# Block attention and soft mixture of experts: scores from four 64x64 parts of the array, in a PSUM layout of fixed bank pairs

## The chip, the cores and the metric

The kernel runs on one core of a Trainium2 chip. The metric is the device time of one execution in microseconds (us). Before the change it is 252.64 us, the median of 3 runs (252.4 to 253.21). The engines have the names of the profile: PE is TensorE's matmul and PEld its weight load, DVE is VectorE, ACT is ScalarE, POOL is GpSimd, SP is SyncE, which issues the transfers (SPq is its queue).

## The reference

Everything is float32. Stage one is attention within chunks of 64 tokens, for 8 batches of 8 heads with 576 tokens and head size 64. Stage two is a soft mixture of 8 experts with 4 slots each on the 4608 token rows of 512.

```python
# attention, per batch, head and chunk of 64 tokens
scores = scale * (q_c @ k_c.T);  scores -= scores.max(-1)
attn = exp(scores) / (sum(exp(scores)) + 1e-9)
x = (attn @ v_c)                      # as rows: (4608, 512)
# soft mixture: 32 slots
logits = x @ phi                      # (4608, 32)
d = softmax of logits over all rows;  slot_input = d.T @ x
slot_out[e] = relu(slot_input[e] @ w1[e]) @ w2[e]
c = softmax of logits over the slots; return c @ slot_out
```

## The kernel before

The order of the work is written out by hand, and every engine takes its instructions in the order of the code. The program puts in the waits: an instruction waits where it touches a tile that another engine still writes or reads, and for a PSUM tile that holds between two readers too.

Stage one goes through 36 steps `t` (9 batches of four pairs of heads; the ninth "batch" is the last 64 tokens of all eight). A step covers 512 tokens of two heads, that is 16 blocks of 64 tokens. Its work is cut into parts that a loop (from `for t in range(NT - 2)` on) runs staggered, so that one pass holds parts of five steps:

- `s1(t)`, scores: 8 matmuls into the PSUM tile `psc` (L193). Keys lie in `qkT` twice, each time with the other head's 64 partitions zeroed (memsets L404 and L405), so one matmul contracts over all 128 partitions and gives both heads' scores of one block. Then DVE: maximum `mx` (L201), subtraction into `sc` (L203).
- every fourth pass, `logits`, `weights`, `sums`: the token logits `pl` of a finished batch (L271), their running maximum `nm_run` (L285, L286), exponentials `eT` (L289), a copy `lT` (L299) and a factor `al` (L294) on ACT.
- `transposes(t + 2)`: 8 transposes of queries and keys into the pair of banks `pqk` (L166), then four copies out into `qkT`: three on ACT (L181), the fourth on DVE (L179).
- every fourth pass, one pass after the logits, `partial`: `pp`, the slots' partial sums (L351), and their addition into `p_run` on DVE (L364).
- `s3(t - 3)`: 4 transposes of the results `x` into `px` (L254), and a copy into `xT`, on DVE (L259) in even steps up to `t` = 28, on ACT (L261) in the others.
- `s2a(t - 1)`: 4 transposes of the exponentials into `pt` (L216), a copy into `at` on ACT (L218).
- in the passes with logits, `natural`: two transposes `pe` (L313, L315), a copy `eN` on ACT (L317), then `cm` and `c_all` on DVE (L328, L329).
- `s1b(t)`: the exponential of the scores on ACT (L208).
- `s2b(t - 2)`: 16 matmuls of 64x64 with the values into the pair of banks `pav` (L234); on DVE the reciprocals `rc` (L241, L242) and the product `x` (L243).

After the loop (34 passes) the last parts follow in an order of their own; then the slots' inputs, the experts' two products (`ph` L571, `po` L603) and the combination (`pf` L638) make the second half. It opens PSUM and most of SBUF anew, and its weights `w` are loaded into buffers that stage one's tiles free.

PSUM has eight banks of 512 floats per partition. Stage one spends them in two pools: four single banks that go round over `psc`, `px`, `pt`, `pl`, `pe` and `pp`, and two pairs that go round over `pqk` and `pav`. Since these two take turns, each of them has in effect one pair.

Of the kernel before, what the change touches and what calls it, by code (L numbers as in the profile page):

```python
# [16 lines left out]
def kernel(  # L17
# [81 lines left out]
    with ExitStack() as actx:  # L99
        ap_ = actx.enter_context(tc.tile_pool(name="attn1", bufs=1))  # L100
        a2 = actx.enter_context(tc.tile_pool(name="attn2", bufs=2))
        ps = actx.enter_context(tc.tile_pool(name="ps", bufs=4, space=PSUM))
        psp = actx.enter_context(tc.tile_pool(name="psp", bufs=2, space=PSUM))

        def bank(name):
            return ps.tile([P, 512], F32, tag="ps", name=name)

        def pair(name):
            return psp.tile([P, 2, 512], F32, tag="psp", name=name)
# [16 lines left out]
        xb = tiles("x", [2, NHP, 2, P], range(2))
        xT = ap_.tile([P, 4, NF, P], F32, name="xT")
        v_sb = tiles("v", [4, 2, VW], range(NV))
        qkT.update(tiles("qkT", [3, BT], [1]))
        atb.update(tiles("at", [4, 2, CH], [1]))  # L130
# [27 lines left out]
        def transposes(u):  # L158

            pt = pair(f"pqk_{u}")  # L160
            for isq in range(2):
                src = qkn[(2 * u + isq) % NQK]
                for a in range(2):
                    for i in range(2):
                        o = P * (2 * a + i)
                        nc.tensor.transpose(  # L166
                            out=pt[:, 1 - isq, o:o + P], in_=src[:, a, P * i:P * (i + 1)], identity=ident)
# [17 lines left out]
        def s1(t):  # L185
            psc = bank(f"psc_{t}")
            qT, kb = qkT[t % 2][:, 0], qkT[t % 2][:, 1:3]

            pv = psc.rearrange("p (m a c x) -> p m c a x", m=2, a=2, c=2)
            for c in range(8):  # L190
                m, c2, r2 = c // 4, c // 2 % 2, c % 2
                o = P * (2 * m + r2) + CH * c2
                nc.tensor.matmul(  # L193
                    pv[CH * r2:CH * (r2 + 1), m, c2],
                    lhsT=qT[:, o:o + CH],
                    rhs=kb[:, :, o:o + CH],
                    start=True, stop=True,
                )
# [2 lines left out]
            nc.vector.reduce_max(mx, pv, axis=AX.X)  # L201
# [1 line left out]
            nc.vector.tensor_tensor(sc.rearrange("p (r x) -> p r x", x=CH), pv,  # L203
# [505 lines left out]
```

## Time and profile before

| | |
|---|---|
| median of 3 runs | 252.64 us (252.4 to 253.21) |
| the profiled execution | 252.33 us, its span 250.2 us |
| granted TensorE clock, mean | 0.975 |
| PE busy | 218.9 us, 87% of the span |
| DVE busy | 167.9 us, 67% |
| ACT busy | 149.4 us, 60% |
| DMA traffic | 71.87 MB, mean 287 GB/s |

The page shows one execution; its span runs from the first instruction to the last, and 2.1 us of the execution's time lie around it. A row of the timeline gives the start in us from the span's start, the duration, the engine and line, and what is written from what; "[0.66 <-DVE x L243]" says that the engine was idle for 0.66 us before, and that the wait ended with DVE's instruction of L243. A group's row gives count, busy time in us and the mean of one instruction in ns. A float32 matmul shows as two records on PE, so 8 matmuls count x16.

### The profile page before, as it was taken

Reading aid. Unit: us, or ns where it says so; the run is one execution under the profiler, and the core shown is the slowest. Engines: PE = TensorE matmul, PEld = TensorE weight load, DVE = VectorE, ACT = ScalarE, POOL = GpSimd, SP = SyncE. Lnnn points to the kernel's source line nnn. Section 1 sums busy time; section 2 is a strip of 40 time slices with the busy share of each in tenths; the row PEclk is TensorE's granted clock in tenths of the full one; section 3 lists DMA queues with packets and bytes.
Section 4 is the critical chain, followed back from the end, with each engine's and each line's share of the span. In section 5 each row is a group of like instructions: output and inputs, shape, how many; then the busy total and the mean of one; then the engine's idle time right before and its main releaser. Section 6 shows DMA issues by size and latency. Waiting matters only on the chain.

```text
span 250.2 us, 7883 instructions
## 1 busy us (share of the span) xinstructions
PE 218.9 (87%) x3199; PEld 162.0 (65%) x3199; DVE 167.9 (67%) x385; ACT 149.4 (60%) x300; POOL 7.1 (3%) x29
## 2 busy tenths in 40 slices
PE   6889889988988988988988988989989999998920
PEld 3667777777777677677677677667543265776910
DVE  4567886995995995995995995987570024654720
ACT  3497876776776786786686686685322124553610
POOL 1000000000000000000000000000031000000000
PEclk9799999999999999999999999999999999999975
DMA  6999999989999699999999888992699999999887
GB/s 196 336 293 261 315 303 249 327 270 229 291 243 274 183 331 255 316 344 263 328 337 337 198 290 234 321 277 65 214 340 348 348 349 349 346 366 337 297 260 272
DMA packets 88947, 71.87 MB, mean 287 GB/s; under 512 B 40784, under 2 KB 84816, under 8 KB 88912
## 3 DMA queue, kind: packets, MB, share of 16 engines
q1 hardware_dynamic: 88912, 71.38, 96.6%
q8 instruction: 25, 0.41, 0.7%
q14 instruction: 10, 0.08, 0.1%
HBM read 61.93 MB, written 9.44 MB: 285 GB/s over the span
## 4 chain that ended last, share of the span: by engine, by line
PE 48%; DVE 25%; ACT 16%; issue 4%; DMA 2%; SPq 1%; ACTq 0%; DVEq 0%
ACT qkT L181 13%; PE pf L638 7%; DVE qkT L179 6%; PE psc L193 6%; PE po L603 6%; PE ph L571 6%; PE pqk L166 6%; DVE x L243 6%; PE pav L234 4%; PE px L254 4%; PE pt L216 3%; DVE xT L259 3%; DVE mx L201 2%; DMA qk_w<-in_q_dram 2%; DVE sc L203 2%
## 5 line engine op out<-in xcount | busy, mean ns | idle before, releaser
L181 ACT COPY qkT<-pqk 64x512 f32<-64x512 f32 x107 | 66.7, 623 | 30.0 <-PE pqk L166 28.3
L166 PE MATMUL pqk<-ident,qk_w 128*128 128x128 f32 x288 | 41.3, 288 | 5.8 <-DVE qkT L179 5.0
L166 PEld LDWEIGHTS pqk<-ident,qk_w 128*128 128x128 f32 x288 | 32.3, 145 | 15.1 <-DVE qkT L179 8.7
L179 DVE COPY qkT<-pqk 64x512 f32<-64x512 f32 x37 | 25.8, 698 | 22.4 <-ACT qkT L181 15.0
L193 PE MATMUL psc<-qkT 128*64 128x128 f32 x576 | 40.1, 282 | 0.8 <-DVE qkT L179 0.8
L193 PEld LDWEIGHTS psc<-qkT 128*64 128x64 f32 x576 | 31.3, 138 | 3.8 <-ACT qkT L181 1.0
L254 PE MATMUL px<-ident,x 128*128 128x128 f32 x144 | 22.9, 283 | 7.4 <-DVE x L243 6.6
L254 PEld LDWEIGHTS px<-ident,x 128*128 128x128 f32 x144 | 15.6, 141 | 18.6 <-DVE x L243 17.5
L234 PE MATMUL pav<-v,at 64*64 64x65 f32 x1152 | 25.3, 224 | 0.5 <-ACT eN L317 0.3
L203 DVE TENSOR_TENSOR sc<-psc,mx 128x512 f32<-128x512 f32 x36 | 24.9, 691 | 1.3
L243 DVE TENSOR_TENSOR x<-pav,rc 128x512 f32<-128x512 f32 x36 | 24.9, 691 | 1.2
L201 DVE TENSOR_REDUCE mx<-psc 128x8 f32<-128x512 f32 x36 | 24.4, 677 | 0.3 <-PE psc L193 0.2
L234 PEld LDWEIGHTS pav<-v,at 64*64 64x64 f32 x1152 | 20.3, 134 | 6.4 <-issue 5.2
L216 PE MATMUL pt<-ident,sc 128*128 128x128 f32 x144 | 21.9, 275 | 1.6 <-ACT sc L208 1.6
L208 ACT ACTIVATE sc<-sc 128x512 f32<-128x512 f32 x36 | 23.0, 639 | 0.3 <-DVE sc L203 0.3
L218 ACT COPY at<-pt 128x512 f32<-128x512 f32 x36 | 21.2, 589 | 1.9 <-PE pt L216 1.5
L638 PE MATMUL pf<-sst,cst 128*128 128x256 f32 x72 | 18.7, 405 | 0.9 <-DVE sst L625 0.9
L638 PEld LDWEIGHTS pf<-sst,cst 128*128 128x128 f32 x72 | 17.4, 329 | 1.9 <-DVE sst L625 1.3
L216 PEld LDWEIGHTS pt<-ident,sc 128*128 128x128 f32 x144 | 16.6, 141 | 2.5 <-ACT sc L208 2.3
L571 PE MATMUL ph<-w,siT 128*32 128x512 f32 x128 | 14.6, 595 | 0.8 <-DVE c_all L329 0.8
L644 DVE COPY ob<-pf 128x512 f32<-128x512 f32 x18 | 12.2, 689 | 4.0 <-PE pf L638 3.9
L642 ACT COPY ob<-pf 128x512 f32<-128x512 f32 x18 | 10.5, 586 | 7.0 <-PE pf L638 6.7
(90 smaller groups left out, 194.8 us busy)
## 6 DMA issues: line engine op xcount, KB each, us to landing
w<-in_moe_w_dram SPq DMA_DIRECT2D x30, 1024.0 KB
qk_w<-in_k_dram SPq DMA_DIRECT2D x32, 256.0 KB
qk_w<-in_q_dram SPq DMA_DIRECT2D x32, 256.0 KB
v<-in_v_dram SPq DMA_DIRECT2D x64, 128.0 KB
out_dram<-ob SPq DMA_DIRECT2D x16, 512.0 KB
qk_w<-in_moe_w_dram SPq DMA_DIRECT2D x2, 1024.0 KB
qk_w<-in_k_dram SPq DMA_DIRECT2D x8, 128.0 KB
qk_w<-in_q_dram SPq DMA_DIRECT2D x8, 128.0 KB
```

The lines of the kernel that those rows point to most:

```text
L166: nc.tensor.transpose(out=pt[:, 1 - isq, o:o + P], in_=src[:, a, P * i:P * (i + 1)], identity=ident)
L179: nc.vector.tensor_copy(o, pv[D * j:D * (j + 1), a])
L181: nc.scalar.copy(o, pv[D * j:D * (j + 1), a])
L193: nc.tensor.matmul(pv[CH * r2:CH * (r2 + 1), m, c2], lhsT=qT[:, o:o + CH], rhs=kb[:, :, o:o + CH], start=True, stop=True,)
L201: nc.vector.reduce_max(mx, pv, axis=AX.X)
L203: nc.vector.tensor_tensor(sc.rearrange("p (r x) -> p r x", x=CH), pv, mx.unsqueeze(2).to_broadcast([P, 8, CH]), ALU.subtract)
L216: nc.tensor.transpose(out=pt[:, P * r:P * (r + 1)], in_=sc[:, r], identity=ident)
L234: nc.tensor.matmul(pav[CH * r2:CH * (r2 + 1), c2, i * VW:(i + 1) * VW], lhsT=at[rs, i, r2, :], rhs=v_sb[t % NV][rs, 2 * m + r2, a, :], sta ...
L243: nc.vector.tensor_tensor(xb[n % 2][:, :, hp].rearrange("p c m (a d) -> p c (m a) d", a=2), av[..., 0:D], rc.to_broadcast([P, 2, 4, D]), A ...
L254: nc.tensor.transpose(out=px[:, P * j:P * (j + 1)], in_=xb[n % 2][:, j % 2, hp, j // 2], identity=ident)
L571: nc.tensor.matmul(ph[SL * i:SL * (i + 1), :], lhsT=siT[:, j, :], rhs=wt[1, e, j // 2][:, j % 2, DM * h:DM * (h + 1)], start=(j == 0), sto ...
L638: nc.tensor.matmul(pf[:, DH * j:DH * (j + 1)], lhsT=cv[:, 2 * j2 + j, :], rhs=sst[h], start=True, stop=True)
```

## The change

Four things change, all in stage one.

1. **Scores in quarters of the array.** A matmul covers one head's block alone: 64 partitions in, 64 columns, 64 wide. It is 16 matmuls in place of 8, each on one of four 64x64 parts. The zeroed copies of the keys and their memsets are gone.
2. **Fixed bank pairs.** PSUM is divided into two single banks (`pt` and `pp`), a pair for `pqk` alone, and two fixed pairs. The pair `mid` (`fix0` in the rows) holds `psc` in its middle and `px` at its two ends. The pair `far` (`fix1`) holds `pav` in its middle, a batch's logits `pl` and the transposed logits at one end, the transposed weights `pe` at the other. The waits go by the whole pair. After the loop the freed banks are given out in pairs (`free`, `spare`).
3. **`xT` in two halves.** Each step's copy from `px` becomes two of 128x256, ACT's first, then DVE's, in every step.
4. **Order.** `s2a(t - 1)` moves ahead of `partial` and `s3(t - 3)`. The tiles of stage one lie in another order in SBUF.

```diff
-        ps = actx.enter_context(tc.tile_pool(name="ps", bufs=4, space=PSUM))
-        psp = actx.enter_context(tc.tile_pool(name="psp", bufs=2, space=PSUM))
+        ps = actx.enter_context(tc.tile_pool(name="ps", bufs=2, space=PSUM))
+        psp = actx.enter_context(tc.tile_pool(name="psp", bufs=1, space=PSUM))
+        psx = actx.enter_context(tc.tile_pool(name="psx", bufs=1, space=PSUM))
...
+        mid, far = (psx.tile([P, 1024], F32, name=f"fix{i}") for i in range(2))
+        psc = mid[:, 256:768].rearrange("p (a x) -> p a x", a=2)
+        px = mid[:, 0:256], mid[:, 768:1024]
+        pav = far[:, 512 - 4 * VW:512 + 4 * VW].rearrange("p (c x) -> p c x", c=2)
+        side = far[:, 0:P], far[:, 1024 - P:1024]
...
-            for c in range(8):
-                m, c2, r2 = c // 4, c // 2 % 2, c % 2
-                o = P * (2 * m + r2) + CH * c2
-                nc.tensor.matmul(
-                    pv[CH * r2:CH * (r2 + 1), m, c2],
-                    lhsT=qT[:, o:o + CH],
-                    rhs=kb[:, :, o:o + CH],
-                    start=True, stop=True,
-                )
+            for i in range(4):
+                m, c2 = divmod(i, 2)
+                for r2 in range(2):
+                    o = P * (2 * m + r2) + CH * c2
+                    for a in range(2):
+                        rs = slice(D * a, D * (a + 1))
+                        nc.tensor.matmul(
+                            psc[CH * r2:CH * (r2 + 1), a, CH * i:CH * (i + 1)],
+                            lhsT=qT[rs, o:o + CH],
+                            rhs=kT[rs, o:o + CH],
+                            start=True, stop=True,
+                        )
...
-            if t == NT - 1 or t % 2 == 0 and t < NT - 6:
-                nc.vector.tensor_copy(o, pv)
-            else:
-                nc.scalar.copy(o, pv)
+            for i, copy in enumerate((nc.scalar.copy, nc.vector.tensor_copy)):
+                copy(xT[:, 2 * i:2 * i + 2, hp], px[i].rearrange("p (j x) -> p j x", j=2))
...
-                pls[b] = bank(f"pl_{b}")
+                pls[b] = side[0]
...
-            pe = bank(f"pe_{b}")
-            nc.tensor.transpose(out=pe[:, 0:P], in_=eT, identity=ident)
+            pe = side[1]
+            nc.tensor.transpose(out=pe, in_=eT, identity=ident)
             if with_l:
-                nc.tensor.transpose(out=pe[:, P:2 * P], in_=lT, identity=ident)
+                nc.tensor.transpose(out=side[0], in_=lT, identity=ident)
...
-        for t in qkT.values():
-            nc.vector.memset(t[0:D, 2], 0.0)
-            nc.vector.memset(t[D:P, 1], 0.0)
...
+            if t >= 1:
+                s2a(t - 1)
             if t % 4 == 0 and t >= 8:
                 partial((t - 8) // 4)
             if t >= 3:
                 s3(t - 3)
-            if t >= 1:
-                s2a(t - 1)
...
+        free.extend(('pqk', ''))
```

What stands in PE's row before, from the scores of step 14 to those of step 15, with the waits that the program carries ("DVE_49" is a count of DVE's finished instructions; "DMAHW" ones are those of transfers):

```order
L193 MATMUL psc_14_1089<-qkT0_93 64x2x64 x8
...
L254 MATMUL px_11_1114<-ident_63,x0_96 128x128 [waits DVE_49]
L254 MATMUL px_11_1114<-ident_63,x0_96 128x128 x3
L216 MATMUL pt_13_1120<-ident_63,sc2_95 128x128 [waits PE_49,Activation_49]
L216 MATMUL pt_13_1120<-ident_63,sc2_95 128x128 x3
L234 MATMUL pav_12_1128<-v0_99,at0_94 64x65 [waits DMAHW1_49,PE_49]
...
L193 MATMUL psc_15_1154<-qkT1_103 64x2x64 x8
```

And the same place now; `fix0` is the pair `mid`, `fix1` the pair `far`, L213 the scores, L272 the results' transposes, L253 the values' products:

```order
L213 MATMUL fix0_96<-qkT0_98 64x64 [waits DVE_49]
L213 MATMUL fix0_96<-qkT0_98 64x64 x15
...
L236 MATMUL pt_13_1204<-ident_63,sc2_106 128x128 [waits Activation_49]
L236 MATMUL pt_13_1204<-ident_63,sc2_106 128x128 x3
L272 MATMUL fix0_96<-ident_63,x0_109 128x128 [waits DVE_49]
L272 MATMUL fix0_96<-ident_63,x0_109 128x128 x3
L253 MATMUL fix1_97<-v0_102,at0_107 64x65 [waits DMAHW1_49]
...
L213 MATMUL fix0_96<-qkT1_99 64x64 [waits DVE_49]
```

The transposes `pt` stand ahead of `px`. The scores, which waited for nothing but their operands, now carry a wait for DVE; its count is that of DVE's half of the copy into `xT` in the pass before. The wait of `px` is now that for DVE's reading of this pass's scores (`sc`).

ACT's row, in the pass with logits of step 15, before:

```order
L289 ACTIVATE eT_2_1186,es_2_1187<-pl_2_1166,nm_run0_72 128x128
L299 COPY lT_2_1189<-pl_2_1166 128x128
L294 ACTIVATE al_2_1191<-nm_run1_73,nm_run0_72 128x1
...
L218 COPY at0_94<-pt_14_1213 128x512
L317 COPY eN_2_1222<-pe_2_1219 128x128
L208 ACTIVATE sc2_95<-sc2_95 128x512
```

And now (L303, L313 and L308 are `eT`, `lT` and `al`; L200 the copies into `qkT`; L238 that into `at`; L275 the half of `xT`; L331 `eN`):

```order
L303 ACTIVATE eT_2_1281,es_2_1282<-fix1_97,nm_run0_72 128x128
L313 COPY lT_2_1284<-fix1_97 128x128
L308 ACTIVATE al_2_1286<-nm_run1_73,nm_run0_72 128x1
L200 COPY qkT1_99<-pqk_17_1289 64x512 x3
L238 COPY at0_107<-pt_14_1302 128x512
L275 COPY xT_100<-fix0_96 128x2x128
L331 COPY eN_2_1316<-fix1_97 128x128
L228 ACTIVATE sc2_106<-sc2_106 128x512
```

In every pass ACT's half of `xT` now stands behind the three copies into `qkT` and behind that into `at`; DVE's half waits for ACT's, since both read `mid`. In the passes with logits, DVE's `cm` and `c_all` read `far` behind ACT's `eN`, and the values' products of that pass wait for `c_all`.

More of the change, by code (lines that the diff above doesn't have):

```diff
@@ L101, with pair @@
         a2 = actx.enter_context(tc.tile_pool(name="attn2", bufs=2))
-        ps = actx.enter_context(tc.tile_pool(name="ps", bufs=4, space=PSUM))
-        psp = actx.enter_context(tc.tile_pool(name="psp", bufs=2, space=PSUM))
-        def bank(name):
-            return ps.tile([P, 512], F32, tag="ps", name=name)
-        def pair(name):
-            return psp.tile([P, 2, 512], F32, tag="psp", name=name)
+        ps = actx.enter_context(tc.tile_pool(name="ps", bufs=2, space=PSUM))
+        psp = actx.enter_context(tc.tile_pool(name="psp", bufs=1, space=PSUM))
+        psx = actx.enter_context(tc.tile_pool(name="psx", bufs=1, space=PSUM))
+        spare = []
+        free = []
+        def bank(name):
+            if free and not spare:
+                tag = free.pop(0)
+                free.append(tag)
+                if tag:
+                    t = pair(tag, name)
+                    spare.extend((t[:, 0], t[:, 1]))
+                else:
+                    spare.extend(ps.tile([P, 512], F32, tag="ps", name=f"{name}_{i}") for i in range(2))
+            return spare.pop(0) if spare else ps.tile([P, 512], F32, tag="ps", name=name)
+        mid, far = (psx.tile([P, 1024], F32, name=f"fix{i}") for i in range(2))
[3 more added lines that the diff above has]
+        side = far[:, 0:P], far[:, 1024 - P:1024]
+        def pair(tag, name):
+            return psp.tile([P, 2, 512], F32, tag=tag, name=name)
         def warm(n, src=ident):
@@ L120, in tiles @@
             return {i: ap_.tile([P] + shape, F32, name=f"{name}{i}") for i in which}
-        qkT = tiles("qkT", [3, BT], [0])
-        atb = tiles("at", [4, 2, CH], [0])
+        qkT = tiles("qkT", [2, BT], range(2))
+        xT = ap_.tile([P, 4, NF, P], F32, name="xT")
+        xb = tiles("x", [2, NHP, 2, P], [1])
+        v_sb = tiles("v", [4, 2, VW], range(NV))
         sc2 = ap_.tile([P, 2, DM], F32, name="sc2")
[L126 to L130, printed above, removed]
+        atb = tiles("at", [2, 2, 2, CH], range(2))
+        xb.update(tiles("x", [2, NHP, 2, P], [0]))
         def load_qk(u):
@@ L158, in transposes @@
         def transposes(u):
-            pt = pair(f"pqk_{u}")
+            pt = pair("pqk", f"pqk_{u}")
             for isq in range(2):
@@ L166, in transposes @@
                         nc.tensor.transpose(
-                            out=pt[:, 1 - isq, o:o + P], in_=src[:, a, P * i:P * (i + 1)], identity=ident)
+                            out=pt[:, isq, o:o + P], in_=src[:, a, P * i:P * (i + 1)], identity=ident)
             dst = qkT[u % 2]
@@ L217, in s2a @@
             at = atb[t % 2]
-            nc.scalar.copy(at.rearrange("p r g x -> p (r g x)"), pt)
+            nc.scalar.copy(at.rearrange("p a m r x -> p (a m r x)"), pt)
             ats[t] = at
@@ L224, in s2b @@
             rc = a2.tile([P, 2, 4, 1], F32, tag="rc", name=f"rc_{t}")
-            pav = pair(f"pav_{t}")
             for i in range(4):
@@ L239, in s2b @@
                         )
-            av = pav[:, :, :4 * VW].rearrange("p c (h x) -> p c h x", x=VW)
+            av = pav.rearrange("p c (h x) -> p c h x", x=VW)
             nc.vector.tensor_scalar_add(rc, av[..., D:D + 1], EPS)
@@ L250, in s3 @@
         def s3(t):
-            px = bank(f"px_{t}")
             n, hp = divmod(t, NHP)
```

28 lines of the change are left out of this document (12 added, 16 removed).

## The prediction

> **What bounds the kernel now.** I read the page first, then the waits by total, then the timeline of one pass of the loop. The page's shares and its clock row:
>
> ```profile
> PE 218.9 (87%) x3199; PEld 162.0 (65%) x3199; DVE 167.9 (67%) x385; ACT 149.4 (60%) x300; POOL 7.1 (3%) x29
> ...
> PEclk9799999999999999999999999999999999999975
> ```
>
> PE looks like the bound at 87%, at a granted clock that stays at nine tenths or more through the loop. The waits (engine and line, what it waited for: us in total, times, longest) say that it isn't so simple:
>
> ```profile
> PEld px L254 <- DVE x L243: 17.5, 23, 1.1
> ...
> DVE qkT L179 <- ACT qkT L181: 15.0, 12, 2.3
> ```
>
> PE stands before the results' transposes because DVE hasn't the results yet, and DVE stands before its quarter of the `qkT` copies because ACT still reads the same bank pair: readers of one PSUM tile take turns. So a pass is a ring of hand-overs, and its time must be read as a chain. The timeline of one plain pass (start, duration, engine, line):
>
> ```profile
> 125.42 0.70 PE L234 MATMUL pav<-v,at 64*64 64x65 f32 x32
> ...
> 126.05 1.09 PE L193 MATMUL psc<-qkT 128*64 128x128 f32 x16
> 126.34 0.59 ACT L218 COPY at<-pt 128x512 f32<-128x512 f32 x1
> 126.35 0.70 DVE L179 COPY qkT<-pqk 64x512 f32<-64x512 f32 x1
> 126.83 0.64 ACT L208 ACTIVATE sc<-sc 128x512 f32<-128x512 f32 x1
> 127.08 0.69 DVE L259 COPY xT<-px 128x512 f32<-128x512 f32 x1
> ...
> 127.11 1.09 PE L166 MATMUL pqk<-ident,qk_w 128*128 128x128 f32 x8
> 127.69 0.16 DVE L241 TENSOR_SCALAR rc<-pav 128x8 f32<-128x8 f32 x1
> ...
> 128.12 0.69 DVE L243 TENSOR_TENSOR x<-pav,rc 128x512 f32<-128x512 f32 x1
> ...
> 128.29 1.91 ACT L181 COPY qkT<-pqk 64x512 f32<-64x512 f32 x3 [0.83 <-PE pqk L166]
> 128.73 0.68 DVE L201 TENSOR_REDUCE mx<-psc 128x8 f32<-128x512 f32 x1
> ...
> 128.87 0.66 PE L254 MATMUL px<-ident,x 128*128 128x128 f32 x4 [0.66 <-DVE x L243]
> ...
> 129.44 0.69 DVE L203 TENSOR_TENSOR sc<-psc,mx 128x512 f32<-128x512 f32 x1
> ...
> 130.23 0.58 ACT L261 COPY xT<-px 128x512 f32<-128x512 f32 x1
> 130.24 0.69 DVE L179 COPY qkT<-pqk 64x512 f32<-64x512 f32 x1
> ...
> 130.52 0.66 PE L193 MATMUL psc<-qkT 128*64 128x128 f32 x8
> ```
>
> Here the scores follow the values' products at once (125.42 to 126.05, 130.52): nothing downstream holds them. The copy out of `px` (127.08 on DVE, 130.23 on ACT) is held by nobody either, since `px` had a bank of its own. The starts of the scores give the passes' lengths:
>
> ```profile
> 18.80 1.09 PE L193 MATMUL psc<-qkT 128*64 128x128 f32 x16
> ...
> 111.47 1.09 PE L193 MATMUL psc<-qkT 128*64 128x128 f32 x16
> ...
> 116.41 1.09 PE L193 MATMUL psc<-qkT 128*64 128x128 f32 x16
> ...
> 122.18 1.09 PE L193 MATMUL psc<-qkT 128*64 128x128 f32 x16
> ...
> 164.12 1.09 PE L193 MATMUL psc<-qkT 128*64 128x128 f32 x16
> ```
>
> A pass with logits takes 4.94 us (111.47 to 116.41), the next one with `partial` 5.77, the two plain ones 3.87 (to 126.05) and 4.47 (to 130.52): 19.05 for four. From pass 3 to the end of the loop (18.80 to 164.12) 31 passes take 145.3 us.
>
> **The change, part by part.** *Scores in quarters.* The values' products already run so: 32 records of 64x64, 65 wide, move PE on by 0.63 us (125.42 to 126.05). I take 0.63 for the scores too, against about 1.02 now (1.09 busy, the next work 0.07 inside it); bounds 0.51 (half of 1.02) and 1.02. That is 0.4 us a pass of PE time, worth something only where PE is waited for. The memsets' loss is hidden by the first loads.
>
> *The pair `mid`.* Now the scores of pass t+1 wait until DVE has read its half of `px`, and that half waits for ACT's, and ACT's stands behind the three `qkT` copies and `at`. But the `qkT` copies wait for `pqk`, and `pqk` stands behind the scores on PE. That closes a ring without a gap. The two half copies aren't in this trace; the nearest are copies of 128x256 out of PSUM, by form:
>
> ```profile
> L616 DVE COPY sp<-po 128x256 f32<-128x256 f32 x2 | 0.8, 424 | 7.1 <-PE po L603 7.1
> ...
> L624 ACT CAST sst<-prs 128x256 fp32r<-128x256 f32 x2 | 0.7, 372 | 0.5 <-PE prs L621 0.5
> ```
>
> I take 0.42 and 0.37 (bounds: half of a whole copy, 0.35 and 0.29; the whole one, 0.69 and 0.58). The ring: scores 0.63; `pqk` to the first copy 1.18 (127.11 to 128.29); three copies 1.94 (to 130.23); `at` 0.49 until the next on ACT (126.34 to 126.83); ACT's half 0.37; to DVE 0.04 (128.29 + 1.91 = 130.20, DVE at 130.24); DVE's half 0.42; to PE 0.06 (126.35 + 0.70, `pqk` at 127.11). Sum 5.13 us for a plain pass, against 4.17 in the mean. Nothing else is later: counted from the scores' start, DVE's `rc`, `x`, `mx` (0.43, 0.61 and 0.71 apart) have it finish `sc` at about 2.3, `px` on PE ends at 3.0, and ACT reaches its half only at 4.24. So moving `pt` ahead of `px` is right for PE, and costs nothing there, but it puts `at` ahead of ACT's half: 0.49 of the ring.
>
> *The pass with logits.* It has its own rows:
>
> ```profile
> 113.69 0.69 DVE L203 TENSOR_TENSOR sc<-psc,mx 128x512 f32<-128x512 f32 x1
> 114.29 0.28 DVE L285 TENSOR_REDUCE rm<-pl 128x1 f32<-128x128 f32 x1
> ...
> 114.61 0.16 DVE L286 TENSOR_TENSOR nm_run<-rm,nm_run 128x1 f32<-128x1 f32 x1
> ...
> 114.86 0.37 ACT L289 ACTIVATE eT<-pl,nm_run 128x128 f32<-128x128 f32 x1 [2.07 <-DVE nm_run L286]
> ...
> 115.56 1.91 ACT L181 COPY qkT<-pqk 64x512 f32<-64x512 f32 x3
> ...
> 118.84 0.28 DVE L328 TENSOR_REDUCE cm<-pe 128x4 f32<-128x128 f32 x1
> 119.15 0.29 DVE L329 TENSOR_TENSOR c_all<-pe,cm 128x128 f32<-128x128 f32 x1
> ```
>
> From the scores' start, `sc` begins at 1.61, `rm` 0.60 later, `nm_run` 0.32 later, `eT` 0.25 later, the `qkT` copies 0.70 later: 3.48 in place of 1.81. Before, that delay ended in the slack of ACT; now it is in the ring. Then 1.94 + 0.49 to ACT's half (5.91), 0.37 + 0.04 to DVE's (6.32), `cm` 0.34 behind it (0.42 less the 0.08 by which DVE's rows overlap), `c_all` 0.31 later and 0.29 long (7.26), and since `far` is one pair, the values' products wait for that: 0.06 + 0.63, and the next scores start at 7.95.
>
> *The pass with `partial`.* DVE adds `p_run` between its `qkT` quarter and its half of `xT`:
>
> ```profile
> 122.56 0.75 DVE L364 SCALAR_TENSOR_TENSOR p_run<-p_run,al,pp 128x512 f32<-128x512 f32 x1
> ```
>
> DVE's quarter starts at 0.63 + 1.18 + 1.95 = 3.76 and takes 0.70, `p_run` 0.75, the half 0.42, the hand-over 0.06: 5.69.
>
> *The sum of the loop.* Of the 31 passes 7 have logits, 7 `partial`, 17 neither: 7 x 7.95 + 7 x 5.69 + 17 x 5.13 = 182.7 us, 37.4 more than now. The first scores, at a clock not yet up, save about 0.6 (their row is below, among the rivals).
>
> *The end of stage one.* Rows of the logits of batch 7, the products of step 33, and the last half of batch 8's logits:
>
> ```profile
> 169.48 1.08 PE L271 MATMUL pl<-xT,phi_sb 128*32 128x128 f32 x32
> ...
> 170.49 0.70 PE L234 MATMUL pav<-v,at 64*64 64x65 f32 x32
> ...
> 177.47 0.65 PE L271 MATMUL pl<-xT,phi_sb 128*32 128x128 f32 x16
> ```
>
> From the scores of step 34 (164.12) these stand at 5.36, 6.37 and 13.35. With fixed pairs: scores of step 35 behind `sc` of 34 at 2.36, `px` behind `sc` of 35 at 4.55, products of 32 at 5.21, their `x` (behind DVE's half of `xT`) done at 7.16, logits 7.22; `rm`, `nm_run`, `eT`, `lT` on their result, products of 33 at 9.58; the products of 34 and 35 each wait for the `x` before (about 2 to 2.7 us a round: 11.5, 14.2); then three rounds of `px`, ACT, DVE at 0.66 + 0.10 + 0.37 + 0.04 + 0.42 + 0.06 = 1.65 bring the last logits to about 19.9. That is 6.5 us later. The second half starts from there and keeps its order; its chain is PE's own work.
>
> The sum against the profiled execution: 252.33 + 37.4 - 0.6 + 6.5 = **295.6 us**. That execution lies 0.3 below the median of the runs shown, less than they differ among themselves, so I leave it at that. A difference of 0.3% is about what a measurement here can tell from none.
>
> [...] The three copies of `qkT` take ACT 1.91 us a pass, more than any PE step. [...]
>
> **The rivals.** *The halves overlap.* They lie in different banks; if DVE's half didn't wait for ACT's, it would start behind DVE's quarter, at 3.76 + 0.70 = 4.46, and the ring would be 4.94: 31 x 0.19 = 6 less, **290 us**. Against it: the program has the wait. Chance 0.06.
>
> *The logits' pass is lighter.* If `c_all` isn't waited for by the products, that pass ends with DVE's half, 6.32 + 0.42 + 0.06 = 6.80: 7 x 1.15 = 8 less, **287.5 us**. Chance 0.12.
>
> *The clock falls.* In the pass with logits PE idles from the end of `pe` (about 4.8) to 7.3, 2.5 us; no gap in this loop is now longer than about 1.1 us (the longest wait for `x`). A row at a low clock, the kernel's first scores:
>
> ```profile
> 8.41 1.63 PE L193 MATMUL psc<-qkT 128*64 128x128 f32 x16 [0.81 <-DVE qkT L179]
> ```
>
> 1.63 against 1.09, half as long again: on products, scores and `pqk` (2.3 us) that is 1.15 a time, with 8 batches 9 us: **305 us**. Chance 0.11. [...]
>
> *The quarters don't overlap.* If the scores still take 1.02, the ring grows by 0.39: 31 x 0.39 = 12, **308 us**. The products' 0.63 speaks against it. Chance 0.03.
>
> *The other side: the ring isn't what comes last.* If the scores in truth start before `xT` is read, the ring of now remains: `pqk`, three copies, DVE's quarter, `pqk`: 1.18 + 1.95 + 0.70 + 0.06 = 3.89. It decides once the copy of `xT` ends 0.96 us earlier than I make it (5.13 less 4.17), or isn't waited for at all. Then plain passes go at 3.9 in place of 4.17, logits' and `partial` ones save 0.4 of PE: 17 x 0.27 + 14 x 0.4 = 10 less, **242 us**. For it: DMA and PE would allow that. Against it: the rows of ACT and DVE are fixed, and DVE's own order alone gives 4.94. Chance 0.03.
>
> **How the numbers follow.** The forecast has the remaining 0.65. The three durations' bounds are -0.08, -0.07 and -0.12, or +0.21, +0.27 and +0.39 a pass; all low together makes 8 us less, and +0.39 alone 12 more. The range 283 to 307 takes in the forecast with these, the first three rivals and leaves out some 0.1. Faster only by the last rival: 0.03; within 0.3% 0.01; slower 0.96.
>
> **What would show it.** In the profile of the changed kernel: scores some 5.1 us apart in plain passes, 8 in those with logits; the scores waiting for DVE's half of `xT`; the products in every fourth pass waiting for `c_all`; PE's scores near 0.63 us; PE's share near 70%; ACT idle before `qkT` for PE. Wrong if the scores follow the products at once, as at 126.05, or if plain passes stay under 4.6 us.

## The result, and the profile after

The changed kernel takes 315.5 us (median of 4 runs, 315.31 to 320.56) against 252.66 (252.4 to 253.21) for the kernel before, run on the same chip: a ratio of 1.247, 95% interval 1.241 to 1.252. Slower was forecast, at 295.6 us and at most 307: the time lies outside the range. Ratios here compare undisturbed executions alone; the profiles of e2_order, e8_quarters and e12_plain below show executions 1.5 to 2% longer than the fastest of their kernel, and only lengths of single passes and rows are read from those three.

The profiled execution took 315.31 us, its span is 313.5. The page's shares of PE and its clock row:

```profile
PE 222.1 (71%) x3775; PEld 163.9 (52%) x3775; DVE 169.9 (54%) x401; ACT 149.2 (48%) x316; POOL 7.1 (2%) x29
...
PEclk9799978998697799999689789999799599999895
```

The shares went as forecast (PE some 70%). The clock row did not: before, every slice of the loop had a nine, now more than a third of all slices fall below it, and the mean granted clock is 0.905 in place of 0.975. The waits by total (us, times, longest):

```profile
ACT qkT L200 <- PE pqk L185: 70.9, 31, 4.4
DVE qkT L198 <- ACT qkT L200: 51.2, 31, 4.9
...
PE fix L213 <- DVE xT L275: 26.9, 24, 1.6
...
PE fix L253 <- ACT sc L228: 20.5, 7, 3.1
```

ACT waits for `pqk` 31 times. The scores (L213) wait for DVE's half of `xT` in 24 passes, all but the seven that follow a pass with logits, and the values' products (L253) wait in the 7 with logits. For these seven the releaser named, ACT's exponential, is done (at 128.89 in the pass below) before `c_all`, whose row ends last. One plain pass of the timeline, in which the clock was full:

```profile
116.85 0.69 PE L213 MATMUL fix<-qkT 64*64 64x64 f32 x32 [0.85 <-DVE xT L275]
...
117.48 1.09 PE L185 MATMUL pqk<-ident,qk_w 128*128 128x128 f32 x8
...
118.66 1.90 ACT L200 COPY qkT<-pqk 64x512 f32<-64x512 f32 x3 [1.80 <-PE pqk L185]
...
120.58 0.58 ACT L238 COPY at<-pt 128x512 f32<-128x512 f32 x1
...
121.06 0.38 ACT L275 COPY xT<-fix 128x256 f32<-128x256 f32 x1
...
121.48 0.42 DVE L275 COPY xT<-fix 128x256 f32<-128x256 f32 x1 [0.19 <-ACT xT L275]
...
121.95 0.69 PE L213 MATMUL fix<-qkT 64*64 64x64 f32 x32 [1.46 <-DVE xT L275]
```

Term by term this is the ring of the prediction: 0.63, 1.18, 1.92, 0.48, 0.42, 0.47; sum 5.10 against 5.13. And the pass with logits that follows, with the end of the `partial` pass behind it:

```profile
125.45 1.86 ACT L200 COPY qkT<-pqk 64x512 f32<-64x512 f32 x3
...
125.92 0.27 PE L329 MATMUL fix<-ident,lT 128*128 128x128 f32 x1
...
127.82 0.38 ACT L275 COPY xT<-fix 128x256 f32<-128x256 f32 x1
...
128.89 0.29 DVE L343 TENSOR_TENSOR c_all<-fix,cm 128x128 f32<-128x128 f32 x1
129.28 0.70 PE L253 MATMUL fix<-v,at 64*64 64x65 f32 x32 [3.09 <-ACT sc L228]
129.77 0.67 PE L213 MATMUL fix<-qkT 64*64 64x64 f32 x32
...
135.38 0.69 PE L213 MATMUL fix<-qkT 64*64 64x64 f32 x32 [1.27 <-DVE xT L275]
```

7.82 us (121.95 to 129.77), forecast 7.95; and 5.61 with `partial` (to 135.38), forecast 5.69. The products do stand behind `c_all` (128.89 + 0.29 = 129.18).

So a loop of 17 x 5.09 + 7 x 7.82 + 7 x 5.61 = 180.5 us was to be had, and the loop took 192.9 (scores of step 3 at 22.64, of step 34 at 215.58). Of the 12.4 us on top, 1.3 lie in the first of these passes (22.64 to 29.00, 6.36 us), whose clock is full: there `pqk` (its row starts at 24.54) waits 1.25 us for DVE's copy out of the one pair. The other 11.1 lie in passes that met a low clock. Read in windows of 0.2 us, the granted clock steps from 1.00 to 0.50 and back; in the loop the low stretches start at 39.19, 52.84, 76.73, 97.21, 104.04, 151.82, 172.31 and 179.13, each distance a multiple of 3.41 (4, 7, 6, 2, 14, 6 and 2 times), and last 3.41 or 6.83. Here are windows laid on that grid, first five around a pass with logits that took 9.36 us, then three around the pass above (window: length, busy time of PE, PEld, DVE, ACT, POOL, granted clock, DMA share, GB/s):

```profile
93.80:97.21 3.41, 1.61 (x80) 1.34 (x77) 2.56 (x6) 1.94 (x4) 0.00 (x0) 1.00 1.01 372
97.21:100.63 3.42, 3.42 (x36) 3.04 (x28) 1.48 (x5) 1.07 (x5) 0.00 (x0) 0.50 0.53 87
100.63:104.04 3.41, 0.97 (x9) 0.73 (x7) 1.52 (x4) 3.13 (x7) 0.00 (x0) 1.00 0.48 149
104.04:107.45 3.41, 3.23 (x70) 3.14 (x71) 1.98 (x6) 0.00 (x0) 0.00 (x0) 0.50 0.12 28
107.45:110.87 3.42, 3.06 (x52) 1.74 (x50) 1.39 (x3) 2.85 (x6) 0.00 (x0) 1.00 0.62 126
...
121.11:124.52 3.41, 2.22 (x69) 1.89 (x70) 3.08 (x9) 0.86 (x3) 0.00 (x0) 1.00 1.03 198
124.52:127.93 3.41, 1.67 (x16) 1.43 (x14) 0.94 (x3) 3.11 (x9) 0.00 (x0) 1.00 0.89 248
127.93:131.35 3.42, 2.07 (x73) 2.03 (x74) 2.27 (x8) 0.96 (x3) 0.00 (x0) 1.00 0.90 311
```

The windows in which PE worked 1.61 (93.80) and 0.97 us (100.63) of 3.41 were each followed by one at half the clock, a low window; after the low windows with 3.42 (97.21) and 3.23 us of work (104.04) the clock read 1.00 again. In the second group PE never fell below 1.67, and the clock held. Five of the seven passes with logits met a low window, and so did some others.

### The profile page after: what moved, and what is told of

Same layout as the page of the kernel before. It is cut to its first block, busy times and chain, and to the rows that moved or that the text cites. A ratio compares the mean times of both kernels' runs of the same rounds, so it can differ in the third digit from the quotient of the medians.

```text
span 313.5 us, 9012 instructions
## 1 busy us (share of the span) xinstructions
PE 222.1 (71%) x3775; PEld 163.9 (52%) x3775; DVE 169.9 (54%) x401; ACT 149.2 (48%) x316; POOL 7.1 (2%) x29
## 4 chain that ended last, share of the span: by engine, by line
PE 46%; ACT 29%; DVE 16%; issue 4%; DMA 1%; ACTq 0%; DVEq 0%
ACT qkT L200 19%; PE pqk L185 13%; PE pf L650 6%; PE fix L213 6%; PE ph L583 6%; PE po L615 5%; ACT at L238 5%; DVE xT L275 4%; PE fix L253 3%; DVE qkT L198 3%; ACT xT L275 2%; DVE x L262 2%; DVE p_run L378 2%; PE fix L285 2%; PE fix L272 2%
## 5 line engine op out<-in xcount | busy, mean ns | idle before, releaser
L200 ACT COPY qkT<-pqk 64x512 f32<-64x512 f32 x107 | 65.6, 613 | 72.7 <-PE pqk L185 70.9
L213 PE MATMUL fix<-qkT 64*64 64x64 f32 x1152 | 27.9, 241 | 28.3 <-DVE xT L275 26.9
L253 PE MATMUL fix<-v,at 64*64 64x65 f32 x1152 | 27.7, 239 | 22.4 <-ACT sc L228 20.5
L213 PEld LDWEIGHTS fix<-qkT 64*64 64x64 f32 x1152 | 23.3, 151 | 32.6 <-DVE xT L275 30.2
L253 PEld LDWEIGHTS fix<-v,at 64*64 64x64 f32 x1152 | 22.6, 147 | 29.0 <-ACT sc L228 21.9
L272 PE MATMUL fix<-ident,x 128*128 128x128 f32 x144 | 23.6, 287 | 10.7 <-DVE sc L223 9.7
L272 PEld LDWEIGHTS fix<-ident,x 128*128 128x128 f32 x144 | 15.8, 143 | 22.6 <-DVE sc L223 15.3
L223 DVE TENSOR_TENSOR sc<-fix,mx 128x512 f32<-128x512 f32 x36 | 24.9, 692 | 1.3
L262 DVE TENSOR_TENSOR x<-fix,rc 128x512 f32<-128x512 f32 x36 | 24.9, 691 | 1.2
L221 DVE TENSOR_REDUCE mx<-fix 128x8 f32<-128x512 f32 x36 | 24.4, 678 | 1.1 <-PE fix L213 1.0
L238 ACT COPY at<-pt 128x512 f32<-128x512 f32 x36 | 21.1, 585 | 5.2 <-PE pt L236 4.4
L275 DVE COPY xT<-fix 128x256 f32<-128x256 f32 x36 | 15.2, 423 | 8.8 <-ACT xT L275 8.8
L583 PE MATMUL ph<-w,siT 128*32 128x512 f32 x128 | 17.5, 695 | 0.8 <-DVE c_all L343 0.8
L275 ACT COPY xT<-fix 128x256 f32<-128x256 f32 x36 | 13.6, 377 | 7.5 <-PE fix L272 7.5
```

The source lines that it names most:

```text
L200: nc.scalar.copy(o, pv[D * j:D * (j + 1), a])
L213: nc.tensor.matmul(psc[CH * r2:CH * (r2 + 1), a, CH * i:CH * (i + 1)], lhsT=qT[rs, o:o + CH], rhs=kT[rs, o:o + CH], start=True, stop=True,)
L238: nc.scalar.copy(at.rearrange("p a m r x -> p (a m r x)"), pt)
L253: nc.tensor.matmul(pav[CH * r2:CH * (r2 + 1), c2, i * VW:(i + 1) * VW], lhsT=at[rs, a, m, r2, :], rhs=v_sb[t % NV][rs, 2 * m + r2, a, :], ...
L262: nc.vector.tensor_tensor(xb[n % 2][:, :, hp].rearrange("p c m (a d) -> p c (m a) d", a=2), av[..., 0:D], rc.to_broadcast([P, 2, 4, D]), A ...
L272: nc.tensor.transpose(out=px[j // 2][:, P * (j % 2):P * (j % 2 + 1)], in_=xb[n % 2][:, j % 2, hp, j // 2], identity=ident)
```

## The experiments

Theory A: the ring of hand-overs in fixed pairs, as forecast, plus a clock that falls because PE idles within it. Rival B: the long passes have another cause (transfers, waits), and the low clock comes with it. Rival C: the quarters, or a single edit, cost by themselves. All times are medians of 4 runs, ratios to the kernel before on the same chip.

**e1_warm**, dummy matmuls in the long gap of the passes with logits; nobody reads what they write:

```diff
             if t % 4 == 3 and t >= 7:
                 natural((t - 7) // 4)
+                warm(12)
```

> The changed kernel with 12 dummy transposing-size matmuls on PE (128x128, about 1.7 us in all) in each pass with logits, behind the transposes of the weights and ahead of the values' products, where PE stands idle for 2.6 us now. They compute nothing that is used. Theory (the 2.6 us gap makes the granted clock fall in five of the seven logits passes, which costs about 12 us in the loop): no scores of a logits pass run at the low clock any more, the passes become 7.8, 5.6 and 5.1 in every round, time 301 to 305 us, mean clock 0.94 or more. Rival (the waits on the far pair alone make these passes longer, and the clock is only an attendant): time stays at 314 to 317 us and the 8.2 and 9.4 us passes stay.

Measured: 309.29 us (308.54 to 309.51), ratio 1.221 (1.216 to 1.226). The products and scores behind the gap run at full clock in every round, the loop takes 185.4; but in three rounds the clock falls earlier, in the logits themselves (passes of 8.97, 9.18 and 8.76 us). So the long gap is not the only idle time that counts. A miss in size by 4 us.

**e2_order**, `s3(t - 3)` ahead of `s2a(t - 1)` again, so that `at` is out of the ring:

```diff
-            if t >= 1:
-                s2a(t - 1)
             if t % 4 == 0 and t >= 8:
                 partial((t - 8) // 4)
             if t >= 3:
                 s3(t - 3)
+            if t >= 1:
+                s2a(t - 1)
```

> The changed kernel with the old order of the parts: the results' transposes and their copies ahead of the scores' transposes and their copy. ACT then copies its half of xT ahead of the copy into at. Theory (the ring scores, pqk, three qkT copies, at, xT on ACT, xT on DVE sets each pass): a plain pass falls by 0.4 to 0.5 us, from 5.09 to 4.6 to 4.7; over 31 passes 12 to 15 us, time 299 to 304 us, unless the clock falls more or less often. Rival (the ring isn't what sets a pass, PE's low clock is): plain passes stay at 5.1 and the time within 3 us of 315.5.

Measured: 307.93 us (305.5 to 310.99), ratio 1.213 (1.204 to 1.222). Plain passes take 4.94 to 4.95, not 4.6 to 4.7: only 0.15 of `at`'s 0.48 is won, since DVE's own order (its `qkT` quarter, then its half) comes next, at the 4.94 that the prediction had worked out for that case. A miss, and one that the prediction's own numbers could have spared.

**e3_pe**, the transposed weights and logits in a single bank that rotates, in place of `far`:

```diff
-            pe = side[1]
-            nc.tensor.transpose(out=pe, in_=eT, identity=ident)
+            pe = bank(f"pe_{b}")
+            nc.tensor.transpose(out=pe[:, 0:P], in_=eT, identity=ident)
             if with_l:
-                nc.tensor.transpose(out=side[0], in_=lT, identity=ident)
+                nc.tensor.transpose(out=pe[:, P:2 * P], in_=lT, identity=ident)
```

> The changed kernel with the transposes of eT and lT back in a single bank of the rotating pool, so that the values' products of a logits pass no longer wait for eN, cm and c_all. Theory: the logits pass falls from 7.8 to about 6.7 (7 passes, 7 to 8 us), and as PE's gap there shrinks from 2.6 to about 1.5 us the clock no longer falls (12 us more): 294 to 298 us. If the clock's falls don't hang on that gap: 307 to 309 us. Rival (the wait for c_all costs nothing, something else in that pass is as late): 314 to 317 us.

Measured: 307.11 us (306.07 to 307.82), ratio 1.212 (1.207 to 1.218). The products no longer wait, and the first round's pass with logits, at full clock, takes 6.53 (46.67 to 53.20) in place of 7.82. In the six other rounds this pass still takes 8.06 to 8.15. From the timeline of one of them:

```profile
118.78 1.94 PE L285 MATMUL fix<-xT,phi_sb 128*32 128x128 f32 x32 [0.34 <-DVE x L262]
120.65 1.80 PE L185 MATMUL pqk<-ident,qk_w 128*128 128x128 f32 x8
...
123.48 0.70 PE L253 MATMUL fix<-v,at 64*64 64x65 f32 x32
```

Logits of 1.94 in place of 1.08 and `pqk` of 1.80 in place of 1.09: low windows, one a round from the second on, 23.9 us apart, which is seven times 3.41. The rounds of this run fell into step with the grid. What the wait gave, the clock took; a miss.

**e4_px**, the results' transposes in a single bank that rotates, so that the scores wait for `xT` no more:

```diff
+            pb = bank(f"px_{t}")
+            px = pb[:, 0:256], pb[:, 256:512]
             for j in range(4):
```

> The changed kernel with px in a single bank of the rotating pool in place of the ends of the scores' pair, so that the scores no longer wait for the copies into xT; the halves of these copies stay. Theory (that wait closes the ring): plain passes fall from 5.09 to about 4.2, the others by 0.7 to 0.9, 25 to 28 us, and less idling of PE lets the clock fall less often: 275 to 291 us. Rival (the quarters of the array or the split copies cost the time, not the shared pair): over 305 us.

Measured: 299.72 us (299.25 to 300.0), ratio 1.183 (1.178 to 1.189), above what was expected, though the ring is broken as the theory has it. Plain passes take 3.42 and 4.01 (before the change 3.87 and 4.47), and the scores follow the products:

```profile
113.21 0.70 PE L253 MATMUL fix<-v,at 64*64 64x65 f32 x32
113.88 0.74 PE L213 MATMUL fix<-qkT 64*64 64x64 f32 x32
```

The wait of the scores for `xT` is thus shown to be what sets 5.09. But passes with logits now take 9.2 to 11.1 and those with `partial` up to 6.81: PE goes fast through the plain passes and then stands, 1.82 us for `x` ahead of the logits and 3.08 ahead of the products, and the mean clock is 0.865, the lowest of all profiles.

**e5_start**, step 1's `pqk` in `far`, which is still unused there:

```diff
-            pt = pair("pqk", f"pqk_{u}")
+            pt = far.rearrange("p (s x) -> p s x", s=2) if u == 1 else pair("pqk", f"pqk_{u}")
```

> The changed kernel with one thing undone at the start: the second step's transposes of queries and keys go into the far pair, which nobody uses before step 2, so that they no longer wait for the copies of the first step's. Theory (with one pair for pqk the second step's eight transposes start 4.7 us behind the first's, and all passes follow): the scores of step 3 start at 18.5 to 19.5 us from the span's start in place of 22.6, and the time falls by 3.5 to 4 us, to 311 to 312. Rival (the first passes wait for the loads, which come when they come): 315 to 316 us.

Measured: 311.17 us (308.7 to 316.25), ratio 1.226 (1.219 to 1.233). The first passes, in the kernel after and then in this one:

```profile
3.68 1.74 PE L185 MATMUL pqk<-ident,qk_w 128*128 128x128 f32 x8 [0.16 <-DMA qk_w<-in_k_dram]
8.39 1.89 PE L185 MATMUL pqk<-ident,qk_w 128*128 128x128 f32 x8 [2.97 <-DVE qkT L198]
...
22.64 0.65 PE L213 MATMUL fix<-qkT 64*64 64x64 f32 x32
```

```profile
3.59 1.94 PE L185 MATMUL pqk<-ident,qk_w 128*128 128x128 f32 x8
6.08 1.82 PE L185 MATMUL fix<-ident,qk_w 128*128 128x128 f32 x8 [0.55 <-DMA qk_w<-in_k_dram]
...
18.73 0.65 PE L213 MATMUL fix<-qkT 64*64 64x64 f32 x32
```

With one pair for `pqk` alone, the second step's transposes waited 2.97 us for the first step's copies; with another place for them, the scores of step 3 stand at 18.73, as before the change (18.80).

**e6_fill**, filler behind the products of every pass (8 matmuls) and in the passes with logits ahead of them (10):

```diff
                 natural((t - 7) // 4)
+                warm(10)
...
                 s2b(t - 2)
+                warm(8)
```

> The changed kernel with dummy matmuls on PE (128x128, computing nothing that is used) in every pass of the loop: 8 behind the values' products, where PE idles 1.4 us in each pass, and 10 more in the passes with logits, where it idles 2.6 us. All waits of the change stay. Theory (its waits alone make passes of 5.1, 5.6 and 7.8 us, and what comes on top is the clock, which falls when too much of a stretch is idle): every round takes 23.6 us, no scores or logits run at the low clock, 299 to 304 us. Rival (passes are longer than reckoned for another reason than the clock): 312 us or more.

Measured: 330.77 us (326.18 to 333.48): slower than without, at a mean clock of 0.976. The scores are never slow now, but 8 such matmuls take 2.05 us where at most 1.5 were free, so the filler itself became part of the ring (passes of 5.43, 9.83 and 6.38 us). It gave the price of a filler, 0.25 us each, for a better dose.

**e9_dose**, that dose, with e5_start's edit: 4 behind the products of passes without logits, 8 ahead of the products of the others:

```diff
                 natural((t - 7) // 4)
+                warm(8)
...
                 s2b(t - 2)
+                if t % 4 != 3:
+                    warm(4)
```

> The kernel after with step 1's pqk in the pair far (as in the run that did this alone, 311.17) and with measured filler on PE: 4 dummy matmuls of 128x128 (0.25 us each in the run with filler, so 1.0 us) behind the products of passes without logits, whose gap there is about 1.5 us, and 8 (2.0 us) between pe and the products of passes with logits, where the gap is 2.6 us. The dummy results are read by nobody. Filler that fits its gap can't shorten the ring by itself. If the clock made the difference between the undisturbed ring (17 x 5.09 + 7 x 7.82 + 7 x 5.61 = 180.5) and the loop measured (192.9), all scores in the loop take 0.69, the loop takes 180 to 182, and the time is 311.2 - 12.4 = 299, range 296 to 302. Rival one: the long rounds had another cause (transfers, waits for semaphores) that comes with the low clock: the loop stays near 190, 308 to 312. Rival two: the filler itself delays what stands behind it: scores at full clock, but passes over 5.2 and 8.0, time above 303.

Measured: 301.43 us (298.88 to 301.78), ratio 1.190 (1.182 to 1.199), in the range that A gave. Its span and mean clock, and the group of its scores (count, busy time, mean in ns, idle time before):

```profile
core 0: 300.0 us, clock 0.962
```

```profile
L213 PE MATMUL fix<-qkT 64*64 64x64 f32 x1152 | 25.8, 228 | 7.7 <-DVE xT L275 4.8 <-DVE sc L223 2.5
```

All scores from step 3 on take 0.67 to 0.70, and no low stretch lies in the loop, which takes 181.8 us (21.70 to 203.47) with every round from the second on alike: 5.10, 7.84, 5.62, 5.25. That is the 180.5 of the undisturbed ring, plus 0.15 where the filler meets the pass behind `partial`. Idle PE, filled with work that nobody needs, shortens the loop by 11 us against the kernel after and by 9 against e5_start (190.5): B falls. The start lost 3 us of what e5_start had won there, since the early passes met a low window once more (scores of step 2 at 1.14 us); 1.2 of these come back in the first pass of the loop (5.16 in place of 6.35).

**e12_plain**, e9_dose without the filler in the passes with logits, the counterpart of e1_warm:

```diff
-                warm(8)
```

> The kernel e9_dose without the 8 dummy matmuls in the passes with logits: 4 behind the products of the other passes stay (nobody reads their results), so the gaps of 1.5 us are filled and the gap of 2.6 us ahead of the products in passes with logits is open again. It is the counterpart of e1_warm, which filled only the long gap. If one gap of 2.6 us is enough for a low clock, products, scores and pqk behind it are slow in most of the seven rounds (products 1.1, scores 1.1, pqk about 1.7 to 1.9 us), the logits ahead of the gap stay at 1.08 in all, and the time is 5 to 8 us above e9_dose: 306 to 309. Rival: the low clock comes from idle time summed over several passes, and with the short gaps filled the long one does no harm: all scores in the loop take 0.69, and the time is within 1.5 us of e9_dose's 301.4. Second rival: it hangs on where the rounds lie against a fixed window of the throttle; then some rounds are slow and others not, at the same gap.

Measured: 311.67 us (307.93 to 314.78), ratio 1.219 (1.210 to 1.227): some 7 us above e9_dose by the ratios, as expected. The logits run at 1.08 in six of seven rounds. Behind the gap, which is the same to 0.01 us in these two rounds, the products do not:

```profile
98.84 0.70 PE L253 MATMUL fix<-v,at 64*64 64x65 f32 x32 [3.09 <-ACT sc L228]
...
122.60 1.14 PE L253 MATMUL fix<-v,at 64*64 64x65 f32 x32 [3.08 <-ACT sc L228]
```

Three rounds of seven are slow, four not. On the grid of that execution:

```profile
94.34:97.75 3.41, 1.42 (x13) 1.18 (x11) 0.91 (x2) 3.34 (x10) 0.00 (x0) 1.00 0.56 151
97.75:101.16 3.41, 2.32 (x75) 2.28 (x76) 2.38 (x7) 0.74 (x4) 0.00 (x0) 1.00 0.11 31
118.23:121.64 3.41, 1.28 (x12) 1.04 (x10) 1.01 (x3) 3.34 (x11) 0.00 (x0) 1.00 0.93 275
121.64:125.06 3.42, 2.46 (x67) 2.38 (x68) 2.01 (x7) 0.57 (x2) 0.00 (x0) 0.50 0.89 306
125.06:128.47 3.41, 3.41 (x19) 2.08 (x17) 1.16 (x2) 1.84 (x3) 0.00 (x0) 0.50 0.72 178
145.53:148.94 3.41, 0.33 (x19) 0.33 (x22) 1.60 (x4) 2.68 (x6) 0.00 (x0) 1.00 0.45 153
148.94:152.36 3.42, 3.42 (x70) 3.30 (x62) 2.35 (x5) 0.00 (x0) 0.00 (x0) 0.50 0.36 81
```

The second rival of that expectation holds: with gaps of 3.09 and 3.08 us it was not the length that decided but how the gap lay on the grid. Split over two windows, it left 1.42 us of work in one (94.34) and the clock stayed; 0.13 earlier in its window, it left 1.28 (118.23) and the clock fell. The second low window here (125.06) follows one with 2.46 us of work, after which the clock stayed at 0.50; after this one, with 3.41, it read 1.00.

**e10_tail**, e9_dose with filler at the end of stage one as well (5, 4, 4, 3 and 2 matmuls in PE's gaps there):

```diff
         s1(t)
+        warm(5)
         s3(t - 4)
...
         shifted(NL - 1)
+        warm(2)
```

> The kernel e9_dose with more filler at the end of stage one: 5, 4, 4, 3 and 2 dummy matmuls in the gaps of PE between the scores of step 35 and the first ph (gaps of 1.6, 1.3, 1.25, 0.9 and 0.8 us in the kernel after). If the second half lost its 3.6 us because PE enters it at a low clock, its ph take 14.6 us in sum as before the change in place of 17.5, and the time is 3 to 5 us below e9_dose: 294 to 296. Rival: the second half is late for its weights, whose buffers come free later in this order: it stays 69 us long, and the time within 1 us of e9_dose.

Measured: 299.98 us (298.36 to 304.63), ratio 1.185 (1.176 to 1.193): 1.5 us below e9_dose, half of the least expected, and the intervals of the two overlap. The groups of `ph`, before the change, after it, and here:

```profile
L571 PE MATMUL ph<-w,siT 128*32 128x512 f32 x128 | 14.6, 595 | 0.8 <-DVE c_all L329 0.8
```

```profile
L583 PE MATMUL ph<-w,siT 128*32 128x512 f32 x128 | 17.5, 695 | 0.8 <-DVE c_all L343 0.8
```

```profile
L591 PE MATMUL ph<-w,siT 128*32 128x512 f32 x128 | 15.4, 623 | 0.0
```

PE still enters the second half at a low clock, in one window of 3.41 us in place of two. The second half (first `ph` to the end) takes 67.1 us, 69.3 in the kernel after and 65.7 before. In the kernel after, 3.2 of the 3.6 us lie between the first `ph` and the first `po` (20.46 us against 17.29), with the clock at half for the first 6.65 us; here, with the first 1.86 us at half, that stretch takes 18.16. So most of the loss goes with the clock; some 0.5 us in later rows stay open. With hardly a low window, the end of stage one (scores of step 34 at 203.32 to `ph` at 231.25) takes 27.9 us, against 20.3 before.

**e7_undo3**, the edits of e3_pe, e4_px and e5_start together; **e11_undo3fill**, the same with filler in the passes with logits, ahead of the logits and of `pe`:

```diff
             s1(t)
             if t % 4 == 3 and t >= 7:
+                warm(6)
                 logits((t - 7) // 4)
...
             if t % 4 == 3 and t >= 7:
+                warm(7)
                 natural((t - 7) // 4)
```

> The changed kernel with all three waits undone together: px and the weights' transposes in single banks of the rotating pool, and the second step's transposes at the start in the far pair. What stays of the change: the scores in quarters, split copies into xT, the order, the logits in the far pair. Theory (the shared pairs cost nearly all): plain passes 3.4 to 4.1 us as in the run with px alone moved, passes with logits near 7 since three users now take turns in two single banks, a round near 20 us; 262 to 274 us. Rival (quarters or split copies cost of themselves): 290 us or more.

> The kernel e7_undo3 (px and pe in rotating single banks, step 1's pqk in far; 288.39) with filler in the passes with logits alone: 6 dummy matmuls ahead of the logits (gap 1.5 us there) and 7 ahead of pe (gap 1.75 us). In that kernel plain passes take 3.42 and 4.01, passes with logits 8.4 to 10.0 and those with partial 5.44 or, at a low clock, 6.3 to 6.65. If the clock makes the spread, passes with logits take 8.4 or less and those with partial 5.44 each time: about 9 us less over seven rounds, 278 to 281. Rival: the spread comes from banks and transfers, and the time stays at 286 to 290. Either way it stays above the kernel before, since logits and partial together take 13.8 in place of 10.7.

Measured: 288.39 us (287.18 to 289.93), ratio 1.139 (1.134 to 1.145), and 297.28 (296.92 to 300.25), ratio 1.179 (1.169 to 1.190). Both misses. In the first, plain passes keep 3.42 and 4.01, but those with logits take 8.4 to 10.0: `px`, `pt`, `pe` and `pp` now share two single banks. In the second the passes with `partial` do take 5.44 almost each time, but the filler took a bank of the same two, and waited for it just where `pe` had waited:

```profile
138.72 1.83 PE L135 MATMUL pd<-ident 128*128 128x128 f32 x14 [1.95 <-ACT at L238]
...
140.69 0.70 PE L253 MATMUL fix<-v,at 64*64 64x65 f32 x32
```

It did hold the clock up (two low stretches in the loop, eight in e7_undo3), but it came on top: passes with logits of 9.8 to 11.6 us.

**e8_quarters**, the kernel before with quarter scores alone: three pairs that rotate over `psc`, `pqk` and `pav`, and the two banks that remain for the rest:

```diff
-        ps = actx.enter_context(tc.tile_pool(name="ps", bufs=4, space=PSUM))
-        psp = actx.enter_context(tc.tile_pool(name="psp", bufs=2, space=PSUM))
+        ps = actx.enter_context(tc.tile_pool(name="ps", bufs=2, space=PSUM))
+        psp = actx.enter_context(tc.tile_pool(name="psp", bufs=3, space=PSUM))
...
-            psc = bank(f"psc_{t}")
+            psc = pair(f"psc_{t}")[:, :, 0:256]
```

> The kernel before with the scores in quarters alone: as many matmuls and the same layout of queries, keys and exponentials as the change, but the old order, whole copies into xT, and no shared pairs; the scores get a pair of their own out of a pool of three pairs, and two single banks are left for px, pt, the logits, pe and pp (the last batch's logits take a pair). Theory (the quarters shorten PE's scores from 1.02 to 0.63 us, which helps where PE is waited for, and the price is two single banks fewer): plain passes 3.9 to 4.3 us, passes with logits and partial sums 0.5 to 1.5 us longer than before; 248 to 264 us. Rival (the quarters themselves are what is slow): 275 us or more.

Measured: 278.98 us (275.0 to 280.53), ratio 1.094 (1.084 to 1.103). A miss: the time is the rival's, though not for its reason. Plain passes take 3.44 and 4.39 against 3.87 and 4.47, in the mean 3.9 as expected of the quarters, so C falls for the quarters as such. Passes with logits lose it, 7.5 to 8.2 against 4.94, and those with `partial` take 5.44 to 6.65 against 5.77:

```profile
127.22 0.33 PE L314 MATMUL pe<-ident,eT 128*128 128x128 f32 x1 [1.90 <-ACT at L219]
```

`pe` waits for the bank that `pt` holds until ACT has copied it. Half of the single banks were the price of the pair.

## Why the prediction was wrong

The direction was right, and so was the mechanism of the waits. *What bounds it:* the ring, its terms, the waits and the three kinds of passes came within 0.04, 0.13 and 0.08 us; e4_px shows that the wait for `xT` closes the ring, and e9_dose that the ring at full clock makes 182 us. The terms of the sum:

| term | forecast | measured | by |
|---|---|---|---|
| start (scores of step 3) | -0.6 | +3.84 | 18.80 to 22.64; undone by e5_start |
| loop at full clock | +37.4 | +35.2 | 180.5 less 145.3; e9_dose 181.8 |
| first pass of the loop | 0 | +1.3 | 6.36 against 5.09, at full clock; 6.35 in e5_start |
| loop, clock | 0 | +11.1 | 192.9 less 180.5 less 1.3; no low stretch in e9_dose's loop |
| end of stage one | +6.5 | +8.3 | 20.3 to 28.6 us; 27.9 in e10_tail |
| second half | 0 | +3.6 | 65.7 to 69.3 us; 67.1 in e10_tail |

*The step that failed most is that of the clock.* The sum put it at nothing; it stood among the rivals, with a chance of 0.11 and 9 us, weighed by the length of one gap: "no gap in this loop is now longer than about 1.1 us", and the new one would be 2.5. The place was right (2.63 us of idle time ahead of the products at 104.22), its length too; the question was wrong. That the clock would most likely hold over such a gap was the author's estimate; no row of before shows it, and here five of the seven passes with logits met a low window. The window with the gap of 2.63 us and 0.97 us of work (100.63) was followed by one, and in the row of 93.80 no gap longer than 1.5 us stands ahead of a low window. The windows show another quantity: how much PE worked within one stretch of 3.41 us on the grid (the low stretches last 3.41 to 3.42 and 6.83 us). Laid over the forecast, such stretches give windows with little work: PE is busy 67% of a plain pass (3.44 of the 5.10 us from 116.85 to 121.95), and a gap of 2.6 us in every fourth leaves at most 0.8 of 3.41. The rival deserved most of the chance, and its price was 11 us in the loop alone.

*"The first scores save about 0.6"* was the second failed step. It costed the scores and forgot that the change takes the second pair away from `pqk` at the start; the order of the two transposes was in the program to be read, and the trace of before had its rows 2.6 us apart (3.60 and 6.15).

*"The second half starts from there and keeps its order"* was true of the order, not of the clock with which PE arrives: `ph` took 17.5 us in place of 14.6, with the clock at half for the first 6.65 us.

*The end of stage one* was mis-sized by 1.8 us. Up to the last logits the forecast was near: it had them 19.9 us behind the scores of step 34, e10_tail with the clock up has them at 19.5 and the kernel after, with a low stretch, at 20.4. From there to the first `ph` it allowed for no change, and 8.15 us passed in place of 6.98. *The rivals:* the halves did not overlap (DVE's row at 121.48 carries its wait of 0.19 us for ACT's), the products did wait for `c_all`, the quarters did overlap (0.63 in place of 1.03), and the ring did come last; so these four fell. With the measured terms in place of its own, the forecast's sum is 252.3 + 3.8 + 35.2 + 1.3 + 11.1 + 8.3 + 3.6 = 315.6.

What stays open: why the fall has no single threshold (a window with 1.61 us of work was followed by a fall in the kernel after, one with 1.42 in e12_plain was not). In the loops of the kernel after, e1_warm, e9_dose and e12_plain, windows without 64x64 matmuls fell with up to 1.40 us of work and held from 1.42 on; each one that fell with more (1.60 to 1.84) had 0.7 to 1.4 us of 64x64 matmuls in it. No run varies the kind of work alone, so the cause is not shown.

No kernel here beat the one before. The nearest is e8_quarters, whose plain passes are faster; its passes with logits wait for a bank for `pe`, and its clock falls as well (mean 0.923 in its profile). No run parts these two.

## What to carry to other kernels

Price a PSUM layout by its rings: write down who must have read a tile before PE may write it again, and add the hand-overs of one turn; that gave each kind of pass here to about 0.1 us. Then lay stretches of 3.41 us, the spacing of the clock's steps here, over the forecast timeline and add up PE's work in each: here, where the change moved PE from 87% to 71%, the lost clock was a term of the sum (11.1 us in the loop) and not a rival, and it reached into a stage that the change does not touch (`ph` took 17.5 us in place of 14.6). A pair given to one purpose is taken from others: look at the first passes and the rare ones, where the rotation was still of use.

## What the runs showed of the hardware

- In windows of 3.41 us laid end to end over the loop of the kernel after (97.21 is the start of one), each window's granted clock reads 1.00 or 0.50. In the loops of the kernel after, e1_warm, e9_dose and e12_plain, laid on each one's grid, no window with more than 1.9 us of PE work was followed by a fall, and all with less than 1.3 were; between them both occurred. Other work shows no such bound: in the loop of e7_undo3 a window with 1.96 us fell (101.72), and in the kernel after, behind the loop, windows with 2.01 (240.57) and 2.48 us (291.77).
- The way back shows no single bound either. In the kernel after, the low windows with 2.34 (76.73), 2.35 (151.82) and, behind the loop, 3.24 us of work (243.98) were followed by another one, those with 2.88 (8.46), 3.19 (179.13) and 3.23 (104.04) by one at 1.00; in e12_plain one with 2.46 (121.64) was followed by another.
- Rounds fell into step with this grid: e3_pe has a low window in six rounds running, each 23.9 us (seven times 3.41) behind the last, and e4_px low stretches of 6.83 us in five (74.14 to 169.72), at the same distance.
- In 64x64 parts the same scores, in twice as many matmuls, moved PE on by 0.63 us (116.85 to 117.48) in place of 1.03 (166.65 to 167.68 before).
